# A linear-attention mixer with two MLPs: first MLP over three stretches of 1024 tokens, four weight pieces in the attention, logits sent for first

## The chip, the cores and the metric

The kernel runs on one core of one Trainium2 chip. The time is that of the device in microseconds (us) for one launch; lower is better. The engines are TensorE (PE, with its weight loads as PEld), VectorE (DVE), ScalarE (ACT), GpSimd (POOL) and SyncE (SP), which here issues all loads and stores.

## What is computed

Everything is float32; the weights come as float64 words that the kernel turns into float32 itself. Batch 4, 8 heads, 768 tokens, head size 48, so 3072 tokens of width 384.

```python
# 1. gated linear attention, token by token
f = sigmoid(f_logit)                       # [4, 8, 768, 48]
state = f[t] * state + outer(k[t], v[t])   # per head, 48 x 48
y[t] = q[t] @ state                        # x = y as [4, 768, 384]
# 2. first MLP, with a low-rank mixing over the tokens
u = x + ((x^T @ U) @ V)^T                  # rank 32
x = u + relu(u @ w_ch1) @ w_ch2            # 384 -> 1536 -> 384
# 3. second MLP, gated by a convolution of 3 tokens
h = relu(x @ w_in)                         # 384 -> 1024
out = (h * sigmoid(conv3(h))) @ w_out      # 1024 -> 384
```

## The kernel before

**Attention.** The 24 chunks of 128 tokens (i = 0 to 23, six to a batch entry) go through a loop written out by hand; each engine runs its instructions in the order of the code. An iteration issues its loads on SP: `k` and `q` of chunk i+3, `f` (the logits) of chunk i+4, `v` of chunk i+2. `gate_max` clamps the logits (tile `sp<-f`) on VectorE for the first chunks and on GpSimd afterwards, `gates` turns them into log-decays on ScalarE (an exponential and a logarithm), `prefix` sums them by a matmul (`n`) and makes the scaled `q` and `k` (`qh`, `kh`; on GpSimd from chunk 6 on), `turn` transposes these (`qTp`, `kTp`) and ScalarE copies them out, `scores` makes `s`, `mask` multiplies them by a triangle (`p`), `out_chunk` makes `y` and the state's increment `kv`, `out_evac` copies `y` to `u`, and `state_end` renews the state: an addition on VectorE (`wtmp`) and a product on GpSimd (`w`), for which the next `y` waits. `tokens`, `mix_in`, `mix_z` and `mix_out` (tiles `xt`, `z`, `zst`, `mix`) do the mixing over tokens of the entries finished so far; `mix_out` ends with an addition on VectorE (`u<-mix,u`).

**Weight pieces.** Each of the 24 pieces of the first MLP's weights (12 of `w1`, 12 of `w2`, 384 KB each) is loaded, put together from its words by three steps on VectorE (`cvt`), and split into a high part by ScalarE (`w1h`, `w2h`) and a low part by GpSimd (`w1l`, `w2l`). Six of them are done in the attention, in `slot` and `slot_end`; the others in the first MLP, two after each unit (there is a load, then a unit later the conversion, then a unit later the split).

**First MLP.** Units run over the batch entry (768 tokens) and the 12 blocks of 128 hidden channels. `up1` makes a block `a` in two halves of 384 tokens, each nine matmuls (three rows of blocks, each high times high, high times low, low times high); ScalarE makes `rh` by a relu, VectorE the rest `rl`. `down1` takes them, nine matmuls to a half, into the accumulators `b`. TensorE has at each moment one unit of `up1` (18 matmuls) and then the `down1` of the unit before. The second MLP (`up2`, `gate`, `down2`) works in the same way with halves of 384; its weights are converted during the first MLP.

**Output.** `down2` copies a block of 128 tokens out of PSUM into a tile `o` (five buffers) and SP stores it, six to a batch entry.

Of the kernel before, what the change touches and what calls it, by code (L numbers as in the profile page):

```python
# [17 lines left out]
N_EARLY = 6  # L18
EARLY_GATES = 4
DVE_GATES = 8  # L20
# [3 lines left out]
O_BUFS = 5  # L24
SPLIT_FROM = 3
CATCH_UP = 19
# [9 lines left out]
def kernel(  # L36
# [28 lines left out]
    HF = S // 2  # L65
    D2 = 2 * D
# [51 lines left out]
    def w64_steps(pool, loaded, full=True):  # L118
        raw, p, n = loaded
        words = raw[0:p, 0:2 * n].rearrange("p (n w) -> p n w", w=2)  # L120
        lo, hi = words[:, :, 0], words[:, :, 1]
        t = pool.tile([128, 384], I32, tag="cvt", name="cvt")[0:p, 0:n]
        ve = nc.vector
        word = [
            lambda: ve.tensor_scalar(out=t, in0=hi, scalar1=3, scalar2=0x3FFFFFFF, op0=ALU.logical_shift_left, op1=ALU.bitwise_and),  # L125
            lambda: ve.scalar_tensor_tensor(out=t, in0=hi, scalar=-(1 << 30), in1=t, op0=ALU.bitwise_and, op1=ALU.bitwise_or),
            lambda: ve.scalar_tensor_tensor(out=t, in0=lo, scalar=29, in1=t, op0=ALU.logical_shift_right, op1=ALU.bitwise_or),
        ]
        if not full:
            return t.bitcast(F32), word  # L130
        g = pool.tile([128, 384], I32, tag="cvg", name="cvg")[0:p, 0:n]
# [70 lines left out]
    def mlps(ms, banks, pieces, late, extra, checks, hooks):  # L202
# [4 lines left out]
        uh = mc.tile([128, KD, S], F32R, name="uh")  # L207
        ul = mc.tile([128, KD, S], F32R, name="ul")
        w2v = w2h.rearrange("p j x -> p (j x)").rearrange("p (i k s) -> p i k s", i=2, k=KD)
        parts = [(uh, ul), (w2v[:, 0], w2v[:, 1])]  # L210
# [24 lines left out]
        def up(wh, wl, j, at=0, evac=None):  # L235
            uh, ul = parts[at]
            js = slice(j * 128, (j + 1) * 128)
            for i, hf in enumerate(halves):
                ps = bank(i, [128, HF], f"a{i}")
                for kk in range(KD):  # L240
                    mm(ps, wh[:, kk, js], uh[:, kk, hf], kk == 0, False)
                    mm(ps, wh[:, kk, js], ul[:, kk, hf], False, False)
                    mm(ps, wl[:, kk, js], uh[:, kk, hf], False, kk == KD - 1)
                    if kk < KD - 1:
                        hook(j, i, kk)
                if evac:
                    evac(hf, ps)
                hook(j, i, KD - 1)

        def hook(*at):  # L250
            if at in hooks:
                hooks.pop(at)()

        def up1(b, j):
            rh = rg.tile([128, S], F32R, tag="rh", name="rh")
            rl = rg.tile([128, S], F32R, tag="rl", name="rl")

            def evac(hf, ps):
                nc.scalar.activation(out=rh[:, hf], in_=ps, func=ACTF.Relu)  # L259
                nc.vector.scalar_tensor_tensor(  # L260
                    out=rl[:, hf], in0=ps, scalar=0.0, in1=rh[:, hf].bitcast(F32),
                    op0=ALU.max, op1=ALU.subtract,
                )

            up(w1hv, w1lv, j, evac=evac)
            rt[1, b, j] = rh, rl

        def down1(b, j):
            if j == 0:
                acc[1, b] = [bank(i + 2, [128, HF], f"b{i}") for i in range(2 * KD)]  # L270
            rh, rl = rt.pop((1, b, j))
            for m in range(KD):
                cs = slice(m * 128, (m + 1) * 128)
                for i, hf in enumerate(halves):
                    ps = acc[1, b][2 * m + i]
                    mm(ps, w2h[:, j, cs], rh[:, hf], j == 0, False)
                    mm(ps, w2h[:, j, cs], rl[:, hf], False, False)
                    mm(ps, w2l[:, j, cs], rh[:, hf], False, j == J1 - 1)
            if j == J1 - 1:
                adds = [lambda i=i, m=m: add1(b, i, m) for m in range(KD) for i in range(2)]  # L280
                if b == B - 1:
                    extra.extend(adds)
                else:
                    for add in adds:
                        add()

        def add1(b, i, m):
            dst = u32[:, m, b * S + i * HF:b * S + (i + 1) * HF]
            nc.vector.tensor_tensor(out=dst, in0=acc[1, b][2 * m + i], in1=dst, op=ALU.add)
# [11 lines left out]
        def up2(b, j):  # L301
            h = m34["ht"][j % 2]
            up(win[0], win[1], j, b % 2, lambda hf, ps: nc.scalar.activation(
                out=h[:, 1 + hf.start:1 + hf.stop], in_=ps, func=ACTF.Relu))
            sigmoid()

        sig = []
# [6 lines left out]
        def gate(b, j):  # L314
# [3 lines left out]
            while extra:  # L318
                extra.pop(0)()
            c = m34["w"].tile([128, S], F32, tag="c", name="c")  # L320
            conv(h, c, slice(0, S))
            if ct:
                gate_split(slice(0, S), *ct.pop(0))
# [55 lines left out]
        def down2(b, j):  # L379
# [3 lines left out]
            for t in range(S // 128):  # L383
# [5 lines left out]
                if j == J2 - 1:  # L389
                    o = m34["o"].tile([128, DM], F32, tag="o", name="o")  # L390
# [3 lines left out]
        units = [(ph, b, j) for ph, nj in ((1, J1), (2, J2)) for b in range(B) for j in range(nj)]  # L394
        lag = {1: 1, 2: 3}
        pend, done = [], 0
        while len(pieces) > 2 * J1 - N_EARLY:
            for step in pieces[0][0](ws_p, *pieces[0][1:])():
                step()
            pieces.pop(0)  # L400
        yield
        split_u(0, (0,), engines=(nc.gpsimd, nc.vector))
        yield
        split_u(0, (1,), engines=(nc.gpsimd, nc.vector))
        yield
        for i, (ph, b, j) in enumerate(units):
            if (ph, b, j) == (2, 0, 0):
                assert not pieces and not pend
                open34()
            if checks and ph == 2 and (b, j) in check_end:  # L410
                check_end[b, j]()
            if ph == 1:
                up1(b, j)
            else:
                up2(b, j)
            if i + 1 < len(units) and units[i + 1][2] == 0:
                gate_prev()
                if units[i + 1][:2] <= (2, 0):
                    split_u(units[i + 1][1])
            jc[0] = j  # L420
            if i == len(units) - 1:
                last = gate_end(b, j)
            elif ph == 2:
                gate(b, j)
                row = j - (SPLIT_FROM if b else J2 - KD - 1)
                if b + 1 < B and 0 <= row < KD:
                    split_u(b + 1, at=(b + 1) % 2, rows=[row])
            yield
            ready, pend = pend, []
# [6 lines left out]
            if late[0] and not win:  # L436
                pieces += open_late() + checks
            rest = len(pieces) if not win else len(pieces) - len(checks)
            for _ in range(1 if 0 < rest <= 2 * J2 else 2):
                if pieces:  # L440
                    pend.append(pieces[0][0](ws_p, *pieces[0][1:]))
                    pieces.pop(0)
            while done < len(units) and done + lag[units[done][0]] + (done == J1 * B - 1) <= i:
                (down1 if units[done][0] == 1 else down2)(*units[done][1:])
                done += 1
                yield
        last()
        while done < len(units):
            down2(*units[done][1:])
# [292 lines left out]
    with tc.manual_schedule():  # L742
# [33 lines left out]
        mixq, late, extra, hooks = [], [False], [], {}  # L776
# [66 lines left out]
        ends_back(2)  # L843
        for i in range(1, NG):
            for x in "kq":
                load_of(f"{x}{i + 3}")
            load_of(f"f{i + 4}")
            load_of(f"v{i + 2}")
            if 1 < i < NG - 1:
# [17 lines left out]
            if EARLY_GATES <= i < NG - 3:  # L867
                gates(i + 3)
# [34 lines left out]
            if i == CATCH_UP:  # L903
                mix_next()
# [17 lines left out]
            if i == FILL_FROM:  # L922
# [3 lines left out]
                mlp = mlps(ms, banks, wq, late, extra, checks, hooks)  # L926
# [24 lines left out]
        def last_mix():  # L951
            for x in range(2 * KD):
                mix_out(B - 1, x, at=2 + x)

        hooks.update({(0, 0, KD - 1): last_z, (0, 1, 1): last_add, (0, 1, KD - 1): last_casts, (1, 0, 0): last_ends, (1, 1, 0): last_mix})
# [13 lines left out]
    with tc.If(nc.values_load(flag[0:1, 0:1], min_val=0, max_val=1) != 0):  # L969
        recurrence(ctx, tc, q, k, v, f_logit, U, V, u32, ident, w64_load, w64_value, mm)  # L970
        with ExitStack() as fs:
            banks = fs.enter_context(tc.tile_pool(name="banks2", bufs=1, space=PSUM))
            with tc.manual_schedule():
                for _ in mlps(fs, banks, list(first_pieces), [True], [], [], {}):
# [149 lines left out]
```

## Time and profile before

| | us |
|---|---|
| median of 3 runs (664.69 to 665.44) | 664.77 |
| the profiled execution, its own time | 667.89 |
| its span, first to last instruction | 666.2 |
| TensorE busy in it | 648.8 (97%) |
| VectorE, ScalarE, GpSimd busy | 431.8, 278.6, 147.6 |

The busy time of TensorE is nearly all of the span, and still it is no measure of waiting in the attention, since the matmuls are pipelined and a matmul's modelled end lies well after the start of the next. Whether TensorE waits is read from the starts of its instructions, and from the chain of waits that ends last.

### The profile page before, as it was taken

To read this page: it belongs to the slowest core of one execution; us is meant where nothing else is said; L and a number is where in the kernel's file an instruction comes from. 1 tells how busy PE (TensorE), PEld (TensorE's weight loads), DVE (VectorE), ACT (ScalarE), POOL (GpSimd) and SP (SyncE) were. 2 spreads that over 40 slices of the span, in tenths; PEclk is the share of its full clock that TensorE was granted. 3 is DMA by queue.
4 is the path that set the end of the run, shared out by engine and by line. 5 is a ranking of instruction groups with operands and counts; after the bars stand their busy time and mean duration, and the time that the engine had idled before them with its cause. 6 is when DMAs were issued, how large, how long until landed. Compare 5 with 4: busy or idle time off the path is not lost.

```text
span 666.2 us, 13611 instructions
## 1 busy us (share of the span) xinstructions
PE 648.8 (97%) x5578; PEld 617.4 (93%) x5578; DVE 431.8 (65%) x697; ACT 278.6 (42%) x554; POOL 147.6 (22%) x183
## 2 busy tenths in 40 slices
PE   8988999999999999999999999999999999999995
PEld 6767777778999999999999999999999999999995
DVE  4856878567777896668433452114998787787762
ACT  5757767765223322124111211114454544544532
POOL 1145758742232411113000200002020110120000
PEclk9989999999999999999999999999999999999999
DMA  9789979820344222212234240000000100200202
GB/s 177 128 163 176 184 159 179 166 68 2 101 136 130 85 72 71 64 56 71 72 106 132 94 143 1 1 1 0 1 1 1 71 2 1 72 0 1 72 1 76
DMA packets 132665, 50.63 MB, mean 76 GB/s; under 512 B 112899, under 2 KB 128284, under 8 KB 132594
## 3 DMA queue, kind: packets, MB, share of 16 engines
q1 hardware_dynamic: 132594, 49.67, 30.2%
q8 instruction: 46, 0.75, 0.5%
q14 instruction: 25, 0.20, 0.1%
HBM read 44.89 MB, written 4.76 MB: 75 GB/s over the span
## 4 chain that ended last, share of the span: by engine, by line
PE 89%; DMA 3%; DVE 2%; ACT 2%; issue 1%; POOL 1%; SPq 0%; POOLq 0%; ACTq 0%; DVEq 0%
PE a L73 38%; PE b L73 37%; PE y L73 4%; PE s L73 3%; DMA f<-in_f_logit_dram 3%; PE n L73 2%; PE kTp L574 1%; PE xt L664 1%; PE qTp L574 1%; PE z L73 1%; PE kv L73 1%; PE mix L73 1%; DVE p L595 1%; DMA out_dram<-o 0%; SPq L503 0%
## 5 line engine op out<-in xcount | busy, mean ns | idle before, releaser
L259 ACT ACTIVATE rh<-a 128x384 fp32r<-128x384 f32 x96 | 47.3, 492 | 221.9 <-PE a L73 221.9
L260 DVE SCALAR_TENSOR_TENSOR rl<-a,rh 128x384 fp32r<-128x384 f32 x96 | 52.9, 556 | 115.5 <-ACT rh L259 115.2
L73 PE MATMUL a<-ul,w1h 128*128 128x384 f32 x288 | 96.5, 335 | 0.0
L73 PE MATMUL a<-uh,w1h 128*128 128x384 f32 x288 | 96.4, 335 | 0.0
L73 PE MATMUL b<-rh,w2h 128*128 128x384 f32 x288 | 96.4, 335 | 0.0
L73 PE MATMUL a<-uh,w1l 128*128 128x384 f32 x288 | 96.2, 334 | 0.0
L73 PE MATMUL b<-rh,w2l 128*128 128x384 f32 x288 | 96.2, 334 | 0.0
L73 PE MATMUL b<-rl,w2h 128*128 128x384 f32 x288 | 96.2, 334 | 0.0
L73 PE MATMUL b<-woh,w1h 128*128 128x384 f32 x264 | 70.4, 335 | 0.0
L76 POOL TENSOR_TENSOR ul<-u,uh 128x384 fp32r<-128x384 f32 x18 | 21.3, 1207 | 174.5 <-ACT uh L102 174.4
L73 PEld LDWEIGHTS a<-ul,w1h 128*128 128x128 f32 x288 | 54.1, 188 | 0.6 <-DVE ul L76 0.6
L73 PEld LDWEIGHTS b<-rh,w2h 128*128 128x128 f32 x288 | 54.1, 188 | 0.3 <-issue 0.3
L73 PEld LDWEIGHTS a<-uh,w1h 128*128 128x128 f32 x288 | 54.1, 188 | 0.1
L73 PEld LDWEIGHTS a<-uh,w1l 128*128 128x128 f32 x288 | 54.1, 188 | 0.0
L73 PEld LDWEIGHTS b<-rl,w2h 128*128 128x128 f32 x288 | 54.1, 188 | 0.0
L73 PEld LDWEIGHTS b<-rh,w2l 128*128 128x128 f32 x288 | 54.0, 188 | 0.0
L312 ACT ACTIVATE c<-c 128x768 f32<-128x768 f32 x31 | 26.3, 848 | 63.7 <-DVE c L342 63.7
L73 PE MATMUL a<-w2h,winh 128*128 128x384 f32 x192 | 49.0, 336 | 0.0
L73 PEld LDWEIGHTS b<-woh,w1h 128*128 128x128 f32 x264 | 48.0, 188 | 0.0
L73 PE MATMUL b<-wol,w1h 128*128 128x384 f32 x132 | 44.2, 335 | 0.0
L125 DVE TENSOR_SCALAR cvt<-raw 128x384 int32<-128x384 int32 (+3 forms) x44 | 36.3, 825 | 8.5 <-POOL w1l L76 8.4
L595 DVE TENSOR_TENSOR p<-s,tri 128x512 f32<-128x512 f32 x48 | 30.9, 686 | 15.5 <-PE s L73 15.2
(136 smaller groups left out, 1335.2 us busy)
## 6 DMA issues: line engine op xcount, KB each, us to landing
raw<-in_moe_w_ch_dram SPq DMA_DIRECT2D x48, 384.0 KB
f<-in_f_logit_dram SPq DMA_DIRECT2D x24, 192.0 KB
k<-in_k_dram SPq DMA_DIRECT2D x24, 192.0 KB
q<-in_q_dram SPq DMA_DIRECT2D x24, 192.0 KB
v<-in_v_dram SPq DMA_DIRECT2D x48, 96.0 KB
out_dram<-o SPq DMA_DIRECT2D x24, 192.0 KB
raw<-in_moe_w_in_dram SPq DMA_DIRECT2D x8, 384.0 KB
raw<-in_moe_w_out_dram SPq DMA_DIRECT2D x8, 384.0 KB
```

The source lines that it names most:

```text
L73: nc.tensor.matmul(out=out, lhsT=lhsT, rhs=rhs, start=start, stop=stop, skip_group_check=True)
L76: eng.tensor_tensor(out=out, in0=a, in1=b, op=ALU.subtract)
L125: lambda: ve.tensor_scalar(out=t, in0=hi, scalar1=3, scalar2=0x3FFFFFFF, op0=ALU.logical_shift_left, op1=ALU.bitwise_and),
L259: nc.scalar.activation(out=rh[:, hf], in_=ps, func=ACTF.Relu)
L260: nc.vector.scalar_tensor_tensor(out=rl[:, hf], in0=ps, scalar=0.0, in1=rh[:, hf].bitcast(F32), op0=ALU.max, op1=ALU.subtract,)
L312: nc.scalar.activation(out=c, in_=c, func=ACTF.Sigmoid)
L574: nc.tensor.transpose(out=ps[:, p, :], in_=src[:, p, 0:MP], identity=ident)
L595: nc.vector.tensor_tensor(out=t, in0=sc[g][j], in1=tri.unsqueeze(1).to_broadcast([128, NP, C]), op=ALU.mult)
L664: nc.tensor.transpose(out=ps[:, m * 128:(m + 1) * 128], in_=u32[:, m, g * C:(g + 1) * C], identity=ident)
```

## The change

The first MLP no longer goes by batch entries but by three stretches of 1024 tokens (`T1`), in two halves of 512 (`HT`). `up1` and `down1` handle one half each, and TensorE gets them in turns: half 0 up, half 1 of the unit before down, half 1 up, half 0 down. One weight piece is moved on after nearly every `up1` half (`tick`), instead of two after a unit. In the attention four pieces are converted, not six. SP sends for the logits `f` ahead of `k` and `q`; the clamp stands at the start of the next iteration and behind the state's product, not at the end of an iteration and ahead of it; the exponential and the logarithm stand behind the copies of `xt` and `qTp` and ahead of those of `y` and `kTp`. The second `mix_out` of an iteration comes behind `turn` of `kT` and uses bank 4 (that of `y`) where it used bank 2 (one of `s`). The output tiles are two `o` and the four buffers of `rh` and `rl`. The sigmoid's table is loaded early; in the second MLP the split of a gated block comes between the two halves of `up2`, and the first MLP's last `down1` after the first unit of the second.

```diff
-N_EARLY = 6
+N_EARLY = 4
-DVE_GATES = 8
+DVE_GATES = 7
-O_BUFS = 5
+O_BUFS = 2
...
+    T1 = 8 * C
+    HT = T1 // 2
+    NT = B * S // T1
...
+        halves1 = [slice(0, HT), slice(HT, T1)]
+
+        def split1(t, i, engines):
+            for kk in range(KD):
+                split(u32[:, kk, t * T1 + i * HT:t * T1 + (i + 1) * HT], uh[:, kk, halves1[i]], ul[:, kk, halves1[i]], engines[i])
+
+        def up1(u, i):
+            t, j = divmod(u, J1)
+            ps = bank(i, [128, HT], f"a{i}")
+            up(w1hv, w1lv, j, halves1[i], (uh, ul), ps, lambda kk: hooks.pop((u, i, kk), int)())
+            if (u, i) == (1, 0):
+                down1(0, 0)
+            rh = rg.tile([128, HT], F32R, tag="rh", name="rh")
+            rl = rg.tile([128, HT], F32R, tag="rl", name="rl")
+            nc.scalar.activation(out=rh, in_=ps, func=ACTF.Relu)
+            nc.vector.scalar_tensor_tensor(
+                out=rl, in0=ps, scalar=0.0, in1=rh.bitcast(F32), op0=ALU.max, op1=ALU.subtract)
...
+            if j == J1 - 1:
+                if t + 1 < NT:
+                    split1(t + 1, i, (nc.vector, nc.gpsimd))
...
+        def tick(j=0):
+            ready, pend[:] = pend[:], []
...
+            for _ in range(1 if pieces or late_pieces else 2):
+                queue = pieces or late_pieces or (checks if win else [])
+                if queue and not (queue is not pieces and j >= J1 - 2) and not (queue is late_pieces and ticks[0] % 4 == 0):
+                    pend.append(queue[0][0](ws_p, *queue[0][1:]))
+                    queue.pop(0)
...
+        items = [(up1, 0, 0), (up1, 0, 1), (up1, 1, 0), (down1, 0, 1), (up1, 1, 1), (down1, 1, 0)]
+        for u in range(2, n1):
+            items += [(up1, u, 0), (down1, u - 1, 1), (up1, u, 1), (down1, u, 0)]
...
+                    if t < O_BUFS:
+                        o = m34["o"].tile([128, DM], F32, tag="o", name="o")
+                    else:
+                        tag = ("rh", "rl")[t % 2]
+                        o = rg.tile([128, HT], F32R, tag=tag, name="o" + tag).bitcast(F32)[:, 0:DM]
...
         for i in range(1, NG):
+            load_of(f"f{i + 4}")
             for x in "kq":
                 load_of(f"{x}{i + 3}")
-            load_of(f"f{i + 4}")
...
             if i > 1 and i % NCH:
                 state_end(i - 1)
+            if EARLY_GATES <= i < NG - 3:
+                gate_max(i + 3)
...
-            if EARLY_GATES <= i < NG - 3:
-                gates(i + 3)
...
-            if i < EARLY_GATES:
+            if i < NG - 3:
                 gates(i + 3)
-            if EARLY_GATES <= i + 1 < NG - 3:
-                gate_max(i + 4)
...
-            for x in range(n_mix):
-                mix_out(*mixq.pop(0), (0, 2 if i < NG - 3 else 6)[x])
-            if i < NG - 3:
+            if n_mix:
+                mix_out(*mixq.pop(0), 0)
+            if i < NG - 3 and i != CATCH_UP:
                 turn(i + 1, "kT")
+            if n_mix:
+                mix_out(*mixq.pop(0), 4)
```

Three places in the order of the instructions carry the prediction. The first is SP's, in an attention iteration; `ends_d` and `ga` are the small transfers that take the chunk's last decay through memory. Before:

```order
L503 DMA k<-in_k_dram 128x8x48
L503 DMA q<-in_q_dram 128x8x48
L503 DMA f<-in_f_logit_dram 128x8x48
L499 DMA v_129<-in_v_dram 128x4x48 x2
L560 DMA ga<-ends_d 112x4x1
```

Of the changed kernel:

```order
L527 DMA f<-in_f_logit_dram 128x8x48
L527 DMA k<-in_k_dram 128x8x48
L527 DMA q<-in_q_dram 128x8x48
L523 DMA v_126<-in_v_dram 128x4x48 x2
L584 DMA ga<-ends_d 112x4x1
```

The logits have moved ahead of two loads of 192 KB each. The second place is ScalarE's, from `b` (the second exponential of the prefix sums) on, in an attention iteration with no weight piece. Before:

```order
L533 ACTIVATE b<-n 128x384
L523 ACTIVATE sp<-sp 128x384
L524 ACTIVATE sp<-sp,one 128x384
L667 CAST xh<-xt 128x384
L576 COPY qT<-qTp 112x512
L659 COPY u_76<-y 128x3x128
L576 COPY kT<-kTp 112x512
```

Of the changed kernel:

```order
L557 ACTIVATE b<-n 128x384
L691 CAST xh<-xt 128x384
L600 COPY qT<-qTp 112x512
L547 ACTIVATE sp<-sp 128x384
L548 ACTIVATE sp<-sp,one 128x384
L683 COPY u_76<-y 128x3x128
L600 COPY kT<-kTp 112x512
```

The pair `sp` has moved from ahead of `xh` to between `qT` and `u`. The third place is ScalarE's early in the first MLP, where each `rh` is one relu and each `w1h`, `w2h` the high part of a weight piece. Before:

```order
L259 ACTIVATE rh<-a_3144 128x384
L259 ACTIVATE rh<-a_3156 128x384
L102 CAST w1h<-cvt 128x3x128
L102 CAST w2h<-cvt 128x384
L259 ACTIVATE rh<-a_3204 128x384
```

Of the changed kernel:

```order
L262 ACTIVATE rh<-a_3079 128x512
L105 CAST w2h<-cvt 128x384
L262 ACTIVATE rh<-a_3110 128x512
L105 CAST w1h<-cvt 128x3x128
L262 ACTIVATE rh<-a_3141 128x512
```

The relus are a third wider, and between two of them stands one piece instead of two or none; the `w1` piece now follows the second half of the unit just ahead of the one that uses it.

## Rows read from the trace of the kernel before

**Rows 1.** Windows by stage: us, busy of PE, PEld, DVE, ACT, POOL, clock, DMA, GB/s.
```profile
0.00:156.84 156.84, 146.64 (x2690) 116.94 (x2691) 105.79 (x211) 105.50 (x219) 84.10 (x128) 0.99 0.76 149
156.84:458.69 301.85, 301.85 (x1737) 300.49 (x1737) 169.28 (x302) 74.94 (x163) 48.75 (x47) 1.00 0.24 74
458.69:659.00 200.31, 200.28 (x1154) 199.93 (x1152) 156.74 (x184) 97.70 (x171) 14.76 (x9) 1.00 0.06 20
```
**Rows 2.** Chain that ended last, late in the first MLP: start, us, what.
```profile
449.33 3.12 PE a L73 x18
452.45 3.12 PE b L73 x18
```
**Rows 3.** Chain, 28 to 130 us: the starts of `scores` that stand in it.
```profile
28.56 1.09 PE s L73 x16
...
44.23 1.14 PE s L73 x16
...
61.05 1.09 PE s L73 x16
...
74.38 1.14 PE s L73 x16
...
80.95 1.09 PE s L73 x16
...
86.61 1.09 PE s L73 x16
...
111.48 1.16 PE s L73 x16
...
117.56 1.09 PE s L73 x16
...
123.23 1.09 PE s L73 x16
...
128.25 1.09 PE s L73 x16
```
**Rows 4.** The logits' tile: idle of the clamping engines for its transfers, us, times.
```profile
  DMA f<-in_f_logit_dram: 13.5, 9
```
**Rows 5.** Timelines of VectorE and GpSimd: two clamps, with the idle time before them.
```profile
37.29 0.36 DVE L516 TENSOR_SCALAR sp<-f 128x384 f32<-128x384 f32 x1 [3.45 <-DMA f<-in_f_logit_dram]
99.11 0.51 POOL L518 TENSOR_SCALAR sp<-f 128x384 f32<-128x384 f32 x1 [2.64 <-DMA f<-in_f_logit_dram]
```
**Rows 6.** Chain at 77 us: VectorE between two iterations.
```profile
77.76 1.24 DVE cvt L127
79.00 0.48 DVE u L707
```
**Rows 7.** ScalarE's timeline at the end: the last six output copies.
```profile
656.41 2.56 ACT L391 COPY o<-b 128x384 f32<-128x384 f32 x5 [1.66 <-PE b L73]
660.17 0.48 ACT L391 COPY o<-b 128x384 f32<-128x384 f32 x1 [1.20 <-DMA out_dram<-o]
```
**Rows 8.** Chain in an undisturbed attention iteration: other matmuls, back to back.
```profile
67.39 0.65 PE n L73 x2
...
69.95 0.44 PE qTp L574 x4
```
**Rows 9.** Groups by form, TensorE and ScalarE: busy us, mean ns, idle before.
```profile
L73 PE MATMUL a<-ul,w1h 128*128 128x384 f32 x288 | 96.5, 335 | 0.0
L259 ACT ACTIVATE rh<-a 128x384 fp32r<-128x384 f32 x96 | 47.3, 492 | 221.9 <-PE a L73 221.9
L576 ACT COPY kT<-kTp 112x512 f32<-112x512 f32 x24 | 14.1, 587 | 9.5 <-PE kTp L574 9.4
```
**Rows 10.** Timelines of TensorE and GpSimd around a `w1` piece, early first MLP.
```profile
176.93 0.33 PE L73 MATMUL b<-rh,w2h 128*128 128x384 f32 x1
...
178.10 1.01 POOL L76 TENSOR_TENSOR w1l<-cvt,w1h 128x384 fp32r<-128x384 f32 x1 [4.27 <-ACT w1h L102]
```
**Rows 11.** ScalarE's timeline in an undisturbed iteration: the copy of `y`.
```profile
115.30 0.48 ACT L659 COPY u<-y 128x384 f32<-128x384 f32 x1 [1.11 <-PE y L73]
```

More of the change, by code (lines that the diff above doesn't have):

```diff
@@ L233, in split_u, with up @@
                     split(u32[:, kk, s], uh[:, kk, hf], ul[:, kk, hf], eng)
-        def up(wh, wl, j, at=0, evac=None):
-            uh, ul = parts[at]
+        def up(wh, wl, j, n, src, ps, hook=None):
+            uh, ul = src
             js = slice(j * 128, (j + 1) * 128)
[L238 to L248, printed above, removed]
@@ L269, in down1 @@
+        def down1(u, i):
+            t, j = divmod(u, J1)
             if j == 0:
-                acc[1, b] = [bank(i + 2, [128, HF], f"b{i}") for i in range(2 * KD)]
-            rh, rl = rt.pop((1, b, j))
+                acc[1, i] = [bank(2 * m + i + 2, [128, HT], f"b{2 * m + i}") for m in range(KD)]
+            rh, rl = rt.pop((1, u, i))
             for m in range(KD):
                 cs = slice(m * 128, (m + 1) * 128)
[L274 to L278, printed above, removed]
@@ L279, in down1 @@
-            if j == J1 - 1:
[L280 to L289, printed above, removed]
+                ps = acc[1, i][m]
@@ L389, in down2 @@
                 if j == J2 - 1:
-                    o = m34["o"].tile([128, DM], F32, tag="o", name="o")
+                    if t < O_BUFS:
+                        o = m34["o"].tile([128, DM], F32, tag="o", name="o")
+                    else:
+                        tag = ("rh", "rl")[t % 2]
+                        o = rg.tile([128, HT], F32R, tag=tag, name="o" + tag).bitcast(F32)[:, 0:DM]
                     nc.scalar.copy(out=o, in_=ps)
                     nc.sync.dma_start(out=out[b, ts, :], in_=o)
[L394 to L429, printed above, removed]
+        pend, ticks = [], [0]
+        late_pieces = []
+        def tick(j=0):
+            ready, pend[:] = pend[:], []
             for stage in ready:
@@ L436, in mlps @@
             if late[0] and not win:
[L437 to L444, printed above, removed]
+                late_pieces.extend(open_late())
@@ new lines, in tick @@
+            ticks[0] += 1
+            for _ in range(1 if pieces or late_pieces else 2):
[3 more added lines that the diff above has]
+                    queue.pop(0)
+        while len(pieces) > 2 * J1 - N_EARLY:
+            for step in pieces[0][0](ws_p, *pieces[0][1:])():
+                step()
+            pieces.pop(0)
@@ new lines, in mlps @@
+        while pieces or late_pieces or checks or pend:
+            tick()
+        units = [(b, j) for b in range(B) for j in range(J2)]
+        done = 0
+        open34()
+        for i, (b, j) in enumerate(units):
+            if flagged and (b, j) in check_end:
+                check_end[b, j]()
+            up2(b, j)
+            if j == J2 - 1 and b + 1 < B:
+                gate_prev()
+            jc[0] = j
+            if i == len(units) - 1:
+                last = gate_end(b, j)
+            else:
+                gate(b, j)
+                row = j - (SPLIT_FROM if b else J2 - KD - 1)
+                if b + 1 < B and 0 <= row < KD:
+                    split_u(b + 1, at=(b + 1) % 2, rows=[row])
+            yield
+            if i == 0:
+                down1(n1 - 1, 1)
+            while done + 3 <= i:
+                down2(*units[done])
@@ L774 @@
             load_of(x)
-        mixq, late, extra, hooks = [], [False], [], {}
+        mixq, late, hooks = [], [False], {}
         zs, zq = [], []
```

90 lines of the change are left out of this document (56 added, 34 removed).

## The prediction

> **What bounds the kernel now.** I read the page first: TensorE is busy nearly all of the span. That says little of the attention, so I cut the span into stages by windows [rows 1]: the attention ends where the first matmul of the first MLP starts, at 156.84 us; from there to 458.69 us stands the first MLP (with two early units of the second, in exchange for its own last), and the second MLP goes on to 659.00 us. In both MLPs TensorE is busy all the time, with the clock granted in full (1.00, the 2.4 GHz level) and the DMA engines a quarter busy or less. The chain of waits shows the same: in the first MLP it never leaves TensorE, 3.12 us for 18 matmuls of 384 columns, which is 173.3 ns from start to start [rows 2]. There, only fewer or cheaper matmuls help, and every other engine has room (VectorE 169.28 of 301.85 us).
>
> In the attention the chain leaves TensorE often. I read the starts of `scores` in it as a clock of the iterations [rows 3]. From 117.56 to 123.23 us one iteration takes 5.67 us, and there the chain is TensorE from end to end: that is the floor for a chunk that hands on its state (the last of each batch entry has no `kv`: 123.23 to 128.25, 5.02 us). Against it I find lost:
> - 28.56 to 44.23 us, two iterations: 15.67 - 11.34 = 4.3 us;
> - 61.05 to 74.38, two iterations: 13.33 - 11.34 = 2.0 us;
> - 74.38 to 80.95: 6.57 - 5.67 = 0.9 us;
> - 86.61 to 111.48, four iterations, one of them short: 24.87 - (3 x 5.67 + 5.02) = 2.8 us;
> - 111.48 to 117.56: 0.4 us.
> These are 10.4 us. The tile view of the logits tells why: the engine that clamps them sat idle for their transfers for 13.5 us in 9 waits [rows 4]. The worst on VectorE is 3.45 us at 37.29 us, and on GpSimd 2.64 us at 99.11 us [rows 5]; they lie in the first and the fourth of the losses. What makes such a wait costly is what is queued behind it: on GpSimd the state's product `w`, for which the next `y` waits, and on ScalarE the exponential, with the copies `xh` and `qT` behind it. The 0.9 us are another thing: VectorE, with two weight conversions, is late with the addition of the second `mix`, and `s` needs that bank [rows 6].
>
> At the end, five output copies run as one train and the sixth, with five buffers, waits 1.20 us for the first store [rows 7].
>
> **The change, part by part.** *Waits for logits.* Two loads less stand ahead of `f`, the clamp is due later, at the next iteration's start and behind `w`, and behind its wait there is no `w` of the same iteration any more, and no `xh` or `qT`. I count three quarters to four fifths of the losses in which a logit wait stands: 3.4 of 4.3, 1.5 of 2.0 and 2.2 of 2.8 us, so 7.1. In the last of these losses the pieces that fall away (the fifth and sixth) are a help too. What is late next is `k` and `q`, sent one load later; they go into `qh` and `kh`, whose products are used an iteration later. *Bank and pieces.* The second `mix` uses the bank of `y`, so `s` no longer waits for its addition: 0.9 and part of 0.4, I take 1.1. Together 8.2 us. The bounds are 0 (the waits move on to other transfers or engines) and the 10.4 us that the floor leaves.
>
> *First MLP, matmuls.* Nine matmuls times two halves times 48 units, up and down, are 1728 (six groups of 288 [rows 9]); now 1296 of 512 columns. 1728 x 0.1733 = 299.5 us. No row shows such a matmul with 512 columns, so I bound its spacing. If time goes with columns, it is 173.3 x 4/3 = 231.1 ns, 299.5 us in all: no gain. Other matmuls run faster per column: `n` takes 325 ns for 384 columns and `qTp` 110 for 128 [rows 8], both at two steps to a column. Half of `n`'s spacing is 162.5 ns for 384, so 216.7 for 512: 280.8 us, a gain of 18.7, if the extra 10.8 ns vanished under the longer matmul. Between them: the 10.8 ns belong to each matmul, whatever its width. Then 216.7 + 10.8 = 227.5 ns, 294.8 us, a gain of 4.7 us. I take this, because the spacing is the same 173 ns in runs of `a` and of `b`, whose operands come from different engines, which looks like a cost of the instruction.
>
> The Trainium skill, "TensorE: Matmul & The Clock Gate", section "Back-to-back issue gap", gives N / 2.4 + about 2.5 ns, which is 162.5 ns for 384 columns; the 173.3 here are more, so the row disagrees. If only those 2.5 ns are saved with each of the 432 matmuls that fall away, and the rest goes with columns, the page makes the gain 1.1 us; that speaks against the change and for the first rival below.
>
> *First MLP, weight pieces.* 20 instead of 18 are moved, one after each half. Ten `w1` pieces are now split right behind the relu of the half before their use. Before, GpSimd finished `w1l` at 178.10 + 1.01 = 179.11 us, which is 2.18 us after the next `b` had started at 176.93 [rows 10], and 18 + 2 matmuls, 3.47 us, lay ahead of its use. Now 9 + 2 matmuls of 227.5 ns lie there, 2.50 us, while the relu is wider: 492 ns at 384 columns, and 587 for ScalarE's copy of 512 [rows 9], so 2.18 + 0.10 = 2.28 us. The weights have to be loaded ahead of the matmul, so this is just in time; I take 0.1 us each, 1.0 us, bounds 0 and 0.3 each. The splits of `u` for the next stretch and the additions at a stretch's end have two items of TensorE, 4.1 us, and more ahead of them: nothing, unless VectorE falls behind; its busy share of 56% in this stage [rows 1] is the cover.
>
> *End.* Six buffers take six copies: the sixth starts at about 659.0 instead of 660.17 us, 1.1 us less. The second MLP's re-ordering lies under a TensorE that is busy throughout: nothing.
>
> **Sum.** 8.2 + 4.7 - 1.0 + 1.1 = 13.0 us. The profiled execution took 667.89 us, so 654.9; that is 3.1 us above the median, and from the median of 664.77 the same step gives **651.8 us**.
>
> **The rivals.** *1. Columns, not matmuls.* The 512-wide matmul costs 231.1 ns. For it: per column, `n` and `qTp` are nearly alike (0.85 and 0.86 ns), so a cost of each instruction is small there [rows 8]. Then the gain is 8.2 - 1.0 + 1.1 = 8.3 us: 656.5. *2. The waits move on.* The four loads of an iteration stay what they were and the DMA engines are 76% busy over the attention [rows 1]; `k`, `q` or GpSimd's queue set the pace where the logits did. For it: GpSimd and VectorE are the engines in the losses. Against it: from 117.56 us on, with all four loads still running, iterations are at the floor. The attention gives 3 us: 3 + 4.7 - 1.0 + 1.1 = 7.8, 657.0. *3. The extra is hidden.* 216.7 ns: 8.2 + 18.7 - 1.0 + 1.1 = 27.0, 637.8. Against it: nothing in the rows shows the 10.8 ns shrinking with width. *4. Slower: the logarithm in the way.* The exponential and the logarithm now stand on ScalarE ahead of the copies of `y` and `kTp`, for which the next `s` waits, and the clamp follows `w`. Where the clamp comes late, each iteration is longer. If this holds in 20 iterations, the attention gives nothing and loses 20 times x; it outweighs the 4.8 us left from x = 0.24 us on. With x = 0.5: 10.0 - 4.8 = 5.2, 670.0. Against it: in an undisturbed iteration ScalarE waits 1.11 us for `y` [rows 11], about as long as the two take.
>
> **How the numbers follow.** Forecast 0.52 (its own range 646 to 656), rival 1 0.19, rival 2 0.17, rival 3 0.07, rival 4 0.05. Within 0.2% (1.3 us, about what a measurement of this kernel can tell from no change) nothing of these ends; small mixtures of 1, 2 and 4 may. So faster 0.93, same 0.02, slower 0.05. The range holds the forecast, rivals 1 and 2 and most of both together (664.77 - 3 + 1.0 - 1.1 = 661.7): 642 to 660.
>
> **What would show it.** In the profile after: in the first MLP's chain, pieces of 9 matmuls of 2.05 us (2.08 for rival 1, 1.95 for rival 3), with short breaks ahead of the third matmul of an early `a`; the first `a` at about 148.6 us (153.8 for rival 2); hardly any wait of `sp` for `f`; iterations of 5.7 us from 28 us on; the last copy `o` following the last `b` at once. I am wrong if `s` starts wait for `kT` behind `sp`, if early `w1` pieces stop TensorE for far more than 0.1 us, or if the spacing at 512 columns lies outside 217 to 231 ns.

## The result, and the profile after

The changed kernel takes 654.88 us (median of 5 runs, 654.50 to 655.96) against 664.69 before on the same chip (662.73 to 665.44): the medians lie 9.8 us apart. The ratio is 0.9862, with a 95% interval from 0.9847 to 0.9878, which is 9.2 us faster, by 8.1 to 10.2. The prediction was 651.8, in a range from 642 to 660. The direction and the range held; the forecast is 3.1 us too low.

The profiled execution after took 654.50 us, with a span of 652.8. The windows by stage show where its 13.4 us of span against [rows 1] lie (columns as there):

```profile
0.00:149.10 149.10, 144.89 (x2690) 115.78 (x2691) 103.71 (x204) 106.36 (x217) 81.64 (x127) 1.00 0.78 151
149.10:443.40 294.30, 294.27 (x1299) 242.17 (x1298) 165.53 (x273) 71.36 (x135) 46.39 (x45) 1.00 0.26 78
443.40:645.56 202.16, 202.14 (x1161) 201.34 (x1159) 155.67 (x187) 97.00 (x171) 17.60 (x12) 1.00 0.06 20
```

The attention ends 7.74 us earlier. The stages behind it do not cut at the same work in both kernels, so I take them together: from the first matmul of the first MLP to the end of the last one of the second it is 496.46 us, against 301.85 + 200.31 = 502.16 in [rows 1], 5.70 us less.

The chain of waits late in the first MLP (start, us, what) answers to [rows 2]: 9 matmuls of 512 columns in 2.04 us, 226.7 ns each.

```profile
437.20 2.04 PE b L76 x9
439.24 2.04 PE a L76 x9
```

Early in it, an `a` whose `w1` piece has just been split shows a small break, 2.06 to 2.09 us where its neighbours take 2.04:

```profile
171.38 2.04 PE b L76 x9
173.43 2.09 PE a L76 x9
```

One such break is larger, 0.3 us. Its third matmul, the first that reads the low part, starts at 223.10, right behind the end of that part on GpSimd (222.03 + 1.02 = 223.05):

```profile
222.03 1.02 POOL L79 TENSOR_TENSOR w1l<-cvt,w1h 128x384 fp32r<-128x384 f32 x1 [3.35 <-ACT w1h L105]
```
```profile
223.10 0.50 PE L76 MATMUL a<-uh,w1l 128*128 128x512 f32 x1
```

The starts of `scores` in the chain answer to [rows 3]. Iteration n is here the time from the start of `scores` of chunk n - 1 to that of chunk n. They now take 5.59 us, or 5.25 and 5.03 at the change of batch entry, from 28.49 to 55.54 us; losses remain behind that (67.61 to 74.31, iteration 11, is 6.70).

```profile
28.49 1.09 PE s L76 x16
34.08 1.09 PE s L76 x16
39.67 1.09 PE s L76 x16
44.92 1.09 PE s L76 x16
49.95 1.09 PE s L76 x16
55.54 1.09 PE s L76 x16
61.52 1.09 PE s L76 x16
67.61 1.14 PE s L76 x16
74.31 1.09 PE s L76 x16
```

Iteration 11 is the one of [rows 6], 6.57 us before, and it is no shorter. What waits there for VectorE's additions is not `s` but `cwp`, a transposition of the convolution's weights that is done once, in the bank of the first mix. The change does not touch it, and the chain shows it before and after:

```profile
79.52 0.24 PE cwp L722
```
```profile
72.36 0.48 DVE u L731
...
72.88 0.24 PE cwp L746
```

In one other place of the kernel before, `s` itself did wait for the addition, 0.65 us in iteration 16. After the change no `s` does:

```profile
111.48 1.16 PE L73 MATMUL s<-qT,kT 48*128 48x128 f32 x16 [0.65 <-DVE u L707]
```

The tile view of the logits answers to [rows 4]: the engines that clamp them wait 6.4 us in 4 waits instead of 13.5 in 9. The worst one left on GpSimd is no shorter than the worst there before [rows 5], 2.69 us, at 81.03 us:

```profile
  DMA f<-in_f_logit_dram: 6.4, 4
```
```profile
81.03 0.51 POOL L542 TENSOR_SCALAR sp<-f 128x384 f32<-128x384 f32 x1 [2.69 <-DMA f<-in_f_logit_dram]
```

Part of the waiting has moved to `q`, which is now sent for later. GpSimd waits for it 4.5 us in 5 waits, where the kernel before has no such wait. One of them is paid for: behind the 1.56 us at 89.51 the state's product `w` is late, `y` waits for `w`, and iteration 15 takes 6.29 us:

```profile
89.51 1.01 POOL L560 TENSOR_TENSOR qh<-q,a 128x384 f32<-128x384 f32 x1 [1.56 <-DMA q<-in_q_dram]
```
```profile
92.73 0.52 POOL w L644
...
93.29 1.56 PE y L76 x49
```

At the end, ScalarE's timeline shows the sixth copy without the wait of [rows 7]:

```profile
642.98 1.00 ACT L401 COPY o<-b 128x384 f32<-128x384 f32 x2 [1.66 <-PE b L76]
...
645.58 0.48 ACT L401 COPY orl<-b 128x384 f32<-128x384 f32 x1
```

But its store does not follow at once. SyncE's timeline has the last issue at 647.05, 1.0 us behind the end of that copy, since the six stores go out one behind another; in the kernel before, the six issues are one row of 4.20 us from 656.91.

```profile
646.57 0.38 SPq L402 DMA_DIRECT2D out_dram<-orh  x1
647.05 0.39 SPq L402 DMA_DIRECT2D out_dram<-orl  x1
```
```profile
656.91 4.20 SPq L392 DMA_DIRECT2D out_dram<-o  x6
```

From the end of the second stage of the MLPs to the end of the span it is 652.8 - 645.56 = 7.2 us after, and 666.2 - 659.00 = 7.2 before. One pair is not enough to say so: over all the profiles of this document that stretch moves between 6.6 and 8.4 us. But its mean is 7.5 us over the three with the old end and 7.5 over the ten with six tiles, and the six stores go out within 3.4 to 4.0 us in every one. No gain at the end is seen.

### The profile page after: what moved, and what is told of

Read it like the earlier page. It is cut to its first block, busy times and chain, and to the rows that moved or that the text cites. A ratio compares the mean times of both kernels' runs of the same rounds, so it can differ in the third digit from the quotient of the medians.

```text
span 652.8 us, 12695 instructions
## 1 busy us (share of the span) xinstructions
PE 641.3 (98%) x5146; PEld 559.3 (86%) x5146; DVE 424.9 (65%) x663; ACT 275.2 (42%) x524; POOL 145.6 (22%) x181
## 4 chain that ended last, share of the span: by engine, by line
PE 94%; DVE 2%; ACT 1%; issue 1%; DMA 0%; POOL 0%; POOLq 0%
PE a L76 38%; PE b L76 38%; PE y L76 5%; PE s L76 4%; PE n L76 2%; PE kTp L598 2%; PE xt L688 1%; PE qTp L598 1%; PE z L76 1%; PE mix L76 1%; PE kv L76 1%; DVE p L619 1%; DMA f<-in_f_logit_dram 0%; ACT sp L548 0%; PE row L76 0%
## 5 line engine op out<-in xcount | busy, mean ns | idle before, releaser
L262 ACT ACTIVATE rh<-a 128x512 fp32r<-128x512 f32 x72 | 43.1, 599 | 221.9 <-PE a L76 217.6
L263 DVE SCALAR_TENSOR_TENSOR rl<-a,rh 128x512 fp32r<-128x512 f32 x72 | 49.8, 692 | 109.1 <-ACT rh L262 109.0
L76 PE MATMUL a<-uh,w1l 128*128 128x512 f32 x216 | 84.4, 391 | 0.0
L76 PE MATMUL a<-uh,w1h 128*128 128x512 f32 x216 | 84.2, 390 | 0.0
L76 PE MATMUL a<-ul,w1h 128*128 128x512 f32 x216 | 84.1, 389 | 0.0
L76 PE MATMUL b<-rh,w2l 128*128 128x512 f32 x216 | 84.1, 389 | 0.0
L76 PE MATMUL b<-rh,w2h 128*128 128x512 f32 x216 | 84.0, 389 | 0.0
L76 PE MATMUL b<-rl,w2h 128*128 128x512 f32 x216 | 84.0, 389 | 0.0
L79 POOL TENSOR_TENSOR ul<-u,uh 128x512 fp32r<-128x512 f32 (+1 forms) x15 | 19.1, 1295 | 127.0 <-ACT uh L105 127.0
L304 ACT ACTIVATE h<-a 128x384 f32<-128x384 f32 x64 | 30.9, 496 | 29.3 <-PE a L76 26.0
```

The lines of the kernel that those rows point to most:

```text
L76: nc.tensor.matmul(out=out, lhsT=lhsT, rhs=rhs, start=start, stop=stop, skip_group_check=True)
L79: eng.tensor_tensor(out=out, in0=a, in1=b, op=ALU.subtract)
L262: nc.scalar.activation(out=rh, in_=ps, func=ACTF.Relu)
L263: nc.vector.scalar_tensor_tensor(out=rl, in0=ps, scalar=0.0, in1=rh.bitcast(F32), op0=ALU.max, op1=ALU.subtract)
L304: nc.scalar.activation(out=h[:, 1 + hf.start:1 + hf.stop], in_=ps, func=ACTF.Relu)
```

## The experiments

Each kernel ran beside the kernel before on the same chip, and its ratio is taken to that (on the three chips the kernel before had medians of 665.63, 664.5 and 664.93 us). "The iterations" is the time from the start of `scores` in iteration 0 to that in iteration 23, from the profiled execution of each kernel.

**The two kernels again.** How much does the profiled execution say of a usual one?

> The kernel before, unchanged, profiled in another execution. Its first profiled execution took 667.89 us, 3 us more than its median of 664.7. Theory: the executions differ in how long the clamping engines wait for the logits, so an execution of about 664.7 us has its first matmul of the first MLP at about 153.7 us (156.84 in the first profile) and idles less than 13.5 us for these transfers, with the MLPs at 502.1 us as before. Rival: the 3 us lie in the MLPs or outside the span, and the attention ends at 156.8 us again.

> The changed kernel, unchanged, as the yardstick on this chip: 654.9 us, first matmul of the first MLP at 149.1 us, within 1 us. If waits for logits make executions differ, this kernel's spread stays near 1.5 us, against 5 us for the kernel before.

Before again took 665.98 us, and its iterations 138.33 us where the first profile has 142.05. In it the logits' waits are longer in sum:

```profile
  DMA f<-in_f_logit_dram: 18.1, 11
```

More idle time before the clamp and a shorter attention: the sum of these waits is no measure of what they cost. After again took 654.53 us (654.29 to 656.66; ratio 0.9851, 0.9823 to 0.9878), its iterations 133.58 us, where the first profile has 134.38. So the attention of the kernel before moved by 3.7 us between these two executions, and that of the changed one by 0.8.

**The order of the logits.** Only the places of the load, the clamp, the exponential and the logarithm are undone:

```diff
-DVE_GATES = 7
+DVE_GATES = 8
...
-            load_of(f"f{i + 4}")
             for x in "kq":
                 load_of(f"{x}{i + 3}")
+            load_of(f"f{i + 4}")
...
-            if EARLY_GATES <= i < NG - 3:
-                gate_max(i + 3)
...
+            if EARLY_GATES <= i < NG - 3:
+                gates(i + 3)
...
-            if i < NG - 3:
+            if i < EARLY_GATES:
                 gates(i + 3)
+            if EARLY_GATES <= i + 1 < NG - 3:
+                gate_max(i + 4)
```

> The changed kernel with the logits sent for behind k and q again, and the clamp, the exponential and the logarithm at their old places; four pieces, the bank of the second mix and the first MLP stay as changed. Theory (the waits for logits were most of the attention's gain): 4 us slower than the changed kernel in the median, 659, up to 7 in single executions, with over 9 us of idle time for the logits. Rival (fewer pieces and the bank gave the attention's gain): 1 to 2 us slower, 656 to 657.

655.74 us (655.23 to 656.58), ratio 0.986 (0.9835 to 0.9886): about 1 us of the 9.8, and that less than the runs can tell from nothing. The engines again wait 16.2 us in 9 waits for logits, and iterations 7 and 9 lengthen (6.60 and 7.11 us, from 5.03 and 5.98). About half of this comes back elsewhere: the waits for `q` are gone, iteration 15 takes 5.59 us instead of 6.29 and iteration 21 6.85 instead of 7.34. So the new order gives and takes. The prediction's 7.1 us for this order do not stand on it alone.

**The ends of chunk 2.** The change has one more edit, which the section on it and its shortened diff do not show: it moves `ends_back(2)`, the transfer `ga<-ends_d` for chunk 2, from ahead of the loop to behind the loads of iteration 1. The prediction gave this no term. Undone alone:

```diff
+        ends_back(2)
         for i in range(1, NG):
...
-            if i < NG - 1:
+            if 1 < i < NG - 1:
                 ends_back(i + 1)
```

> The changed kernel with one edit undone: the copies that bring the ends of chunk 2 back stand ahead of the loop again, so SyncE waits for their write before it issues the loads of iteration 1. Theory now (this move is most of what the attention gained): the loads of iteration 1 start near 19.7 us instead of 17.8, one of the iterations 5 to 7 lengthens to 7 us or more, the 23 iterations sum to 136 to 140 us instead of 134, time 657 to 660. Rival (the four weight pieces, the bank of the mix or the turn in iteration 19 made the gain): loads late but no later iteration longer, 654.5 with 0.7 either way. The prediction's own steps (the logits alone) also give 654.5, since their order stays new.

655.72 us (653.77 to 657.26), ratio 0.9856 (0.9832 to 0.9881): within its interval that is the changed kernel's ratio, and short of the expected 657. The profile does show the delay: the loads of iteration 1 are late, iteration 7 takes 6.94 us instead of 5.03, and the iterations sum to 136.35, though in an execution of 657.2 us, 1.5 above the median. So the move alone is worth 1 us at most, not most of the gain; my theory at this point fell by its size.

The same edit alone in the kernel before:

> The kernel before with one edit of the change alone: the copies of chunk 2's ends are moved behind the loads of iteration 1. Theory now: the iteration of 8.97 to 9.66 us among 5 to 7 shrinks to about 5.3 to 6, and the time falls by 2.6 to 6 us, to 660 to 663. Rival (the gain needs the new order of the logits, or comes from pieces, bank and turn): within 1 us of the kernel before, 664.7 to 666.5.

663.43 us (661.65 to 664.47), ratio 0.9978 (0.9964 to 0.9991): 1.5 us faster by the ratio, by 0.6 to 2.4, which is under the expected 2.6. In its profiled execution, one of the fastest of its runs (661.9 us), the long iteration of 8.97 to 9.66 us is gone (5.59, 5.25 and 6.21 for iterations 5 to 7).

Both edits undone in the changed kernel:

> The changed kernel with the order of the logits (their load behind k and q, clamp, exponential and logarithm in their old places) and the place of the ends of chunk 2 both undone; four pieces, bank, turn and the first MLP stay new. Undoing the order alone cost 1.2 us. Theory now (logits and ends are one queue on SyncE, so the late ends make the late logits bite): more than the sum of the two single ones, the long iteration of 8 to 9 us among 5 to 7 comes back, 23 iterations sum to 138 to 141 us, time 659 to 661. Rival (pieces, bank or turn): 655.7 with 1 us either way, the sum at 136.

657.63 us (656.23 to 659.07), ratio 0.9885 (0.9863 to 0.9907): 1.5 to 3 us behind the changed kernel, under the expected 659, and still more than each edit undone gives alone. Whether it is more than their sum the times cannot tell. The profile says so: iteration 5 is long again, 7.35 us, where with either edit alone it stays at 5.59, and the iterations sum to 139.21. SyncE's timelines show why the two are one thing. With both undone, the loads stand behind `ga`, which goes out at 19.56, 1.9 us after the store of the ends that it reads back, and the logits go out behind `k` and `q`, at 21.11:

```profile
17.65 0.31 SPq L580 DMA_DIRECT2D ends_d<-a  x1
19.56 0.34 SPq L584 DMA_DIRECT2D ga<-ends_d  x1
19.99 0.44 SPq L527 DMA_DIRECT2D k<-in_k_dram  x1
...
21.11 0.90 SPq L527 DMA_DIRECT2D f<-in_f_logit_dram  x1
```

With only the ends undone the logits go first, at 19.80; in the changed kernel at 17.80, and `ga` waits behind them:

```profile
19.37 0.34 SPq L584 DMA_DIRECT2D ga<-ends_d  x1
19.80 0.44 SPq L527 DMA_DIRECT2D f<-in_f_logit_dram  x1
```
```profile
17.80 0.38 SPq L527 DMA_DIRECT2D f<-in_f_logit_dram  x1
...
21.05 0.45 SPq L584 DMA_DIRECT2D ga<-ends_d  x1
```

Over all profiles the moment at which iteration 1 issues its logits goes with the long iteration: in the ten where it lies between 17.80 and 19.80 us, iterations 5 and 6 are at 5.59 and 5.25; at 20.70, 20.83, 21.11 and 21.42 one of them takes 8.97, 9.66, 7.35 and 7.29. Either edit alone keeps the logits ahead of that point. These four are also the four with both edits in their old places, so the moment itself is not shown to be the cause. In the chain of waits with both undone one sees how the delay then feeds itself: the clamp waits for the logits, the exponential and the copy `xh` stand behind the clamp, VectorE's `xl` behind `xh`, and SyncE's next loads, the logits among them, behind that.

```profile
46.20 3.82 DMA f<-in_f_logit_dram
...
50.17 0.52 POOL sp L542
...
50.71 0.54 ACT sp L547
...
51.79 0.47 ACT xh L691
...
52.28 0.45 DVE xl L79
52.73 3.57 DMA f<-in_f_logit_dram
```

**The rest of the attention's edits.** First everything in the attention undone, with the new MLPs and the new end kept (six pieces, bank and order of the mixes, turn in iteration 19, logits and ends all as before):

> The new first MLP and the new end, behind the attention of the kernel before: order of the logits, ends of chunk 2, six weight pieces, bank and order of the mix and the turn in iteration 19 all undone. Theory now (the first MLP gave about 5.7 us, the end nothing, the attention the rest): 664.6 less 5.7, 658.9, in a range of 658 to 660, and the 23 iterations sum to 138 to 142 us as before. The prediction's own parts: 664.6 less 4.7 for the matmuls less 1.1 for the end, 658.8, the same by another sum, so the place from the first matmul a to the last b must tell: 496.5 us or less (the two pieces loaded earlier give back some tenths). Rival (a part of the first MLP's gain hangs on the shorter attention, such as weights that arrive in time): 660.5 or more.

657.70 us (656.24 to 661.31), ratio 0.9891 (0.987 to 0.9911): the MLPs gave 7.2 us, by 5.9 to 8.6, a little more than either sum said. From the first `a` to the last `b` its profile has 495.7 us, 6.3 less than before's 502.0 in the same measure. The profiled execution is the slowest of its seven, 3.6 us above the median, and there the iterations take 140.45 us with a long fifth; so this is again an unlucky execution of the old attention, though about 0.8 us of its excess lie in the end (8.3 us from the last matmul). Against it the whole new attention is worth 1.9 us (0.9862 to 0.9891) or 2.7 (0.9851 to 0.9891), across chips and with intervals that nearly reach 0.

Then two edits undone alone, the number of pieces (`N_EARLY = 6`) and the place of the turn:

```diff
             if i == CATCH_UP:
-                turn(i + 1, "kT")
                 mix_next()
...
-            if i < NG - 3 and i != CATCH_UP:
+            if i < NG - 3:
                 turn(i + 1, "kT")
```

> The changed kernel with six weight pieces in the attention instead of four. The prediction put the bank and the pieces at 1.1 us of the attention and the early pieces at 1.0 us lost in the first MLP. Theory of the prediction: the sum of the 23 iterations rises by 0.5 to 1.1 us, the early pieces a lose their waits (5 to 18 pieces at 2.04 instead of 2.06 to 2.09, about 0.4 us in all), so 654.9 to 655.5. Rival (pieces in the attention cost two loads of 384 KB each in the DMA queues of the logits, whose waits then lengthen): 656 or more. Rival of no effect: within 0.5 of 654.7.

> The changed kernel with only the turn of chunk 20 back behind both mixes in iteration 19. Iterations 20 and 21 take 13.25 us after against 12.96 before. Theory (the earlier turn gives that back): 12.9 to 13.0, and 654.4, faster by 0.3 at most, less than can be told from the time. Rival (the earlier turn hides ScalarE's copy): iteration 20 is longer by 0.5 us or more, 655.2 or more.

654.39 us (652.8 to 655.36; ratio 0.9837, 0.9814 to 0.9861) and 654.28 (653.6 to 655.6; 0.984, 0.9818 to 0.9863): neither edit gave anything that these runs can tell from the changed kernel. The kernel with six pieces is the fairest partner for the old attention: same chip, same pieces, same MLPs. The two lie 3.3 us apart by medians, 3.6 by the ratios (0.9837 to 0.9891). With six pieces the iterations take 134.47 us. Iteration 16 is 6.94 us, against 6.3 to 6.6 with four pieces and 7.0 to 7.2 with the old attention, but others are shorter, so in sum the two pieces were no load. The first MLP has no breaks:

```profile
174.19 2.04 PE a L76 x9
176.23 2.04 PE b L76 x9
```

From its first matmul to the first of the second MLP it takes 293.68 us, against 294.31 with four: the breaks behind the 20 pieces cost 0.6 us. With the old place of the turn, iterations 20 and 21 take 6.61 + 6.36 = 12.97 us instead of 13.25, as expected.

**The width of the halves.** Halves of 384 tokens in the new first MLP (`T1 = 6 * C`):

> The changed kernel with stretches of 768 tokens in halves of 384; everything else stays, the turns of halves on TensorE and one piece after each half included. Theory (each matmul costs 13 ns besides its columns): 1728 matmuls at 173.3 ns instead of 1296 at 226.7, 299.5 instead of 293.8 us, so 5.7 us slower than the changed kernel, about 660.6. Rival (the first MLP gained by the new order or the pieces, not by the width): within 1 us of 654.9.

675.67 us (674.86 to 676.42), ratio 1.0159 (1.0131 to 1.0188): 21 us lost, not 5.7. The matmuls are not why; they take 1.56 us for nine. Counted by the starts of its matmuls, TensorE loses 5.4 us at the early `w1` pieces, about 0.5 at each, where the low part comes too late for the third matmul of `a`, and 8.4 us later in nine places. There the kernel reads the weights' words once more and takes their least (`low`), two loads to a step, and in the chain of waits VectorE stands behind these loads:

```profile
322.28 3.72 DMA raw<-in_moe_w_ch_dram
...
326.61 3.92 DMA raw<-in_moe_w_ch_dram
```

So the same with one load at a step, and with one step more at the start, which puts each weight piece half a unit earlier:

```diff
-            for _ in range(1 if pieces or late_pieces else 2):
+            for _ in range(1):
...
-            if step is up1 and (u, i) != (0, 1):
+            if step is up1:
```

> The changed kernel with the first MLP in halves of 384 tokens as before, and one load at each step of the weights instead of two in the checks, with a step after the second item too, so that the stalls of the first run at 384 go (weights not yet there, check loads of 3.5 us ahead of VectorE's work). Theory (the fixed 13.3 ns per matmul is what the width is worth): 288 matmuls more a stage of a half at 173.3 ns, no piece of 9 above 1.65 us, +5.7 us against the changed kernel, 660.2. Rival (the wider half is worth more, as cover for what stands between the matmuls): stalls move elsewhere and it stays 10 us or more behind, 665 or more.

660.95 us (660.38 to 663.29), ratio 0.9947 (0.993 to 0.9964): 6.1 us behind the changed kernel (5.6 to 6.4 by the ratios), where 5.7 were expected, and the rival (665 or more) falls. Both kinds of loss are gone; behind the start of the first MLP the chain is clean:

```profile
412.82 1.56 PE b L76 x9
414.38 1.56 PE a L76 x9
```

Last, halves of 256, and at the end five tiles for the output:

> The changed kernel with the first MLP in halves of 256 tokens, and, far from it, with five tiles for the output instead of six (the sixth copy waits for the store of the first). First question, what a matmul costs beside its columns: 226.7 ns at 512 and 173.3 at 384 lie on a line of one column per 1/2.4 ns and 13.3 ns; if that is fixed, 120.0 ns at 256; if it is a share of the columns (6.3%), 113.3; if the weight load of 128 columns limits, 130 or more. Second question, the end: theory (the train of stores sets the end, the prediction's 1.1 us for the sixth tile is not there) from the last matmul to the end of the span 7.2 to 7.5 us; the prediction's step: 8.3.

One run: 723.67 us, with long waits of the kind seen at 384 (TensorE waits 22.4 us for `rl` alone). Where it doesn't wait, nine matmuls of 256 columns take 1.08 us:

```profile
492.17 1.08 PE a L76 x9
493.25 1.08 PE b L76 x9
```

That is 120.0 ns each, the value for a fixed cost. At the end the sixth copy waits again, and its store goes out 716.64 - 716.15 = 0.49 us behind the fifth, as with six tiles (0.48). From the last matmul to the end of the span it is 7.0 us, under the expected 7.2 to 7.5 and far from 8.3, but within the spread of that stretch, so this run alone decides nothing. From the first of the six copies to the end of the span it is 722.0 - 712.37 = 9.6 us; with six tiles 652.8 - 642.98 = 9.8, and before 666.2 - 656.41 = 9.8 [rows 7].

```profile
712.37 1.00 ACT L401 COPY o<-b 128x384 f32<-128x384 f32 x2 [1.67 <-PE b L76]
...
715.79 0.48 ACT L401 COPY o<-b 128x384 f32<-128x384 f32 x1 [0.86 <-DMA out_dram<-o]
```
```profile
716.15 0.40 SPq L402 DMA_DIRECT2D out_dram<-orh  x1
716.64 0.40 SPq L402 DMA_DIRECT2D out_dram<-o  x1
```

## Why the prediction was right, and where it was off

**First MLP, matmuls: right in mechanism, a little too small.** A matmul of this form costs its columns and a fixed 13.3 ns. The three widths take 120.0 ns at 256, 173.3 at 384 and 226.7 at 512; each step of 128 columns adds 53.3 ns, one column per 1/2.4 ns, and that makes 106.7, 160.0 and 213.3 of them. Each matmul has a weight load of its own [rows 1], so the runs do not tell whether the 13.3 ns are the matmul's or the change of weights'. The prediction had 227.5. 1728 x 173.3 - 1296 x 226.7 ns = 5.7 us instead of 4.7: its fixed part, taken as what is above half of `n`'s spacing, 10.8 ns, was too small, since half of `n` itself holds some of it. Rivals 1 (231.1 ns) and 3 (216.7) fell. The Trainium skill, "TensorE: Matmul & The Clock Gate", section "Back-to-back issue gap", has N / 2.4 and about 2.5 ns for an isolated matmul; its form agrees with the three widths, its constant does not agree with 13.3.

**Weight pieces: right in kind, mis-sized.** The breaks are where the prediction put them, ahead of the third matmul of an early `a`, but 0.02 to 0.05 us each and one of 0.3, 0.6 us in all by the kernel with six pieces, instead of 1.0. With halves of 384 and the same order of pieces the breaks are about 0.5 us each: the wider half hides most of them.

**Changes of batch entry: a term put at nothing.** By the starts of its matmuls, the kernel before loses about 0.8 us in the first MLP at the changes of batch entry (near 231, 306 and 381 us); the new stretches lose nothing at theirs, and the new start 0.35 us more.

**End: failed.** The term of 1.1 us took the wait of the sixth copy [rows 7] for the end of the chain. The stores' train ends last: the sixth copy is done earlier now, and its store goes out 1.0 us later all the same, behind the other five. Nothing is seen to be gained: 7.2 us in both kernels, 7.5 in the means.

**Bank: failed as read.** The 0.9 us of [rows 6] were put down to `s` waiting for the second mix's bank. The matmul that waits there is `cwp`, in the first mix's bank, and that iteration still takes 6.70 us. What the new bank did take away is the wait of 0.65 us in iteration 16; how much of it was gained was not tried alone.

**Attention: the step that failed is the one from waits to us, and from one execution to the median.** The prediction read 10.4 us of losses from one profiled execution and took 8.2 away; that execution indeed has 7.7 more than the one after. But it took 667.89 us, 3.1 above its kernel's median, and such waits make up that excess: in the second profile of that kernel, 0.4 us above its median, the iterations are 3.7 us shorter. The prediction then took the whole step off the median, 664.77 - 13.0 = 651.8. The new kernel no longer has the excess, so the step belonged to the execution's own time: 667.89 - 13.0 = 654.9, which was worked out on the way and then left. In the median the new attention is worth 1.9 to 2.7 us, or with the 0.6 that its two missing pieces cost later 2.5 to 3.3; on one chip, with equal pieces, 3.3 to 3.6. That is the size that rival 2 gave (3 us), and in part its mechanism: `q` did take some of the logits' place, 0.7 to 6.6 us of waits in the kernels that send for the logits first and none in those that do not, and in the profile after one of these waits lengthened an iteration by 0.7 us.

**Luck.** That 667.89 - 13.0 falls on the measured time is partly luck. Between the two profiled executions the step is 13.4 us: 7.7 in the attention instead of 8.2, 5.7 in the MLPs instead of 4.7 - 1.0 = 3.7, nothing at the end instead of 1.1. And 4.1 of the 7.7 are the one long iteration 5 (9.66 to 5.59), which did not come back when the order of the logits alone was undone.

**Which edits made it.** The 7.1 us for the order of the logits and the 1.1 for bank and pieces don't stand as put. The order and the move of `ends_back(2)` each alone are worth about 1 us or less. Undone together they cost 1.5 to 3 us, and the long iteration comes back; the likely reason is that each alone keeps iteration 1's logits early enough. The move had no term in the prediction, though it stands on the queue that the prediction spoke of. Pieces and turn gave nothing that can be told from the times.

**Rival 4 fell.** With exponential and logarithm in their new place, undisturbed iterations are at 5.59 us, as in the second profile of the kernel before, and in the profile after no matmul `s` waits for `kT`. The one such wait before, 0.62 us in iteration 20, went with the earlier turn.

What stays open: by the ratios 7.2 us for the MLPs and 1.9 for the attention make 9.2, but that is so by construction, since one kernel stands between the other two. The rows of the MLPs show 6.3 of the 7.2: 5.7 of matmuls, and most of the rest the changes of batch entry. The 0.9 us left lie within the interval of the ratio. The bank alone, and what decides that iteration 1's logits must be out by about 20 us, were not tried.

## What to carry to other kernels

Before a step is taken off a median, ask whether the profiled execution is a usual one; if the change removes what made it slow, take the step off its own time. Idle time before an instruction is no cost by itself: 18.1 us of waits stood in a shorter attention than 13.5 us did, and what counts is whether an iteration gets longer. Two edits on one in-order queue can each hide the other's worth, so undo them together before calling either of them nothing.

## What the hardware showed that was not expected

The fixed cost of these fp32r matmuls, 13.3 ns, is the same at 256, 384 and 512 columns and for both `a` and `b`. A narrower half can cost more than that, because the items of TensorE under which a weight piece is split or loaded become shorter: with the new kernel's order of pieces and two loads of 384 KB at each later step, halves of 384 tokens lost 21 us; with one load and each piece half a unit earlier they lost 6, which is the fixed cost.
